# W_in's first half requested earlier, W_spatial later: a newly planned order for a linear-attention and gated-MLP kernel

## The chip, the core and the metric

The kernel runs on one core of a Trainium2 chip. The core has a tensor engine (PE) that does the matmuls, a vector engine (DVE), a scalar engine (ACT), a general engine (POOL) and a sync engine (SP), and it moves data with 16 DMA engines. Each engine works through its own list of instructions in order. The metric is the device time of one launch in microseconds (us). A profile of one execution shows when each instruction ran and what it waited for.

## The reference

`q`, `k`, `v` are (4, 8, 768, 64) in fp32: 4 batches, 8 heads, 768 positions of 64 values. The first part is a linear attention with decay, in blocks of 64 positions; its output is the input of the second part, an MLP whose gate mixes positions.

```python
# attention, per block of 64 positions; state is one 64x64 matrix per head
intra = (qb @ kb.T * Dmask) @ vb                 # Dmask[i, j] = lam**(i-j) for i >= j, else 0
inter = (qb * lam**(pos+1)) @ kv_state
out   = intra + inter
kv_state = lam**64 * kv_state + (kb * lam**(63-pos)).T @ vb
# MLP; x is the attention output as (4, 768, 512)
h = max(x @ w_in, 0)                             # w_in (512, 1024)
u, v = h[..., :512], h[..., 512:]
v_n = (v - mean(v)) / sqrt(var(v) + 1e-6)        # over the 512 features
v_s = w_spatial @ v_n + b_spatial                # w_spatial (768, 768), mixes positions
out = (u * v_s) @ w_out                          # w_out (512, 512)
```

## The kernel before

The work is cut into 12 steps, three per batch; a step is 256 positions of all 8 heads. Every instruction group has a short name, and one list, `ORDER`, written out ahead by a planner, gives the order in which the groups are issued. A token such as `PV.0.1.2.T` is a group (`PV`), its arguments (step 0, part 1, PSUM bank 2) and the engine (T is PE, D is DVE, A is ACT, P is POOL, S is SP). The list is read from left to right and each group goes to the end of its engine's list, so the order on one engine is the order of its tokens. Engines wait for one another only where data or buffers require it. The code of the groups is the same in both kernels; only `ORDER` differs.

The groups that the text speaks of, with the number of the step as n:

- `LQ.n`, `LK.n`, `LV.n` (line 192): SP loads q, k or v of a step, 512 KB each. Each has three buffers (`q_in`, `k_in`, `v_in`, chosen by n modulo 3), so step 3 writes the buffer of step 0.
- `QM.n.x`, `KM.n.x` (289): multiply q or k by powers of lam into bf16 `qc` and `kc`, one half of the heads each, on DVE or POOL. `VC.n` (177, 179 or 181): converts v to bf16. The powers come from `LL` (218, DVE) and `LX` (222 and 223, ACT), and these from `LB` (212, PE) and `LN` (215, ACT).
- `TQ`, `TK` (319): transposes on PE; `EQ`, `EK` copy them out of PSUM. From step 5 on transposing DMAs (`DQ`, `DK`, 306 and 302) do this.
- `SC` (349) scores, `MK` (354) masking on DVE, `KV` (366) state update, `SS` copy of the state, `AV` (387 and 396) attention output in two parts, `FN` a copy of one element that orders the engines, `EX` copies the output, transposed, to `xT`.
- `PV` (421) projects to the second half of W_in's columns, `EV` (426 or 428) applies max, `BN` (436, 437), `RA`, `RD`, `RB` (441, 446, 451) and `VN` (457 or 460) normalise. `PU` (472) and `EU` do the first half of the columns.
- `WT.k.i` (484) transposes W_spatial on PE, where i = 0 reads what `WS.0` loads and i = 1 what `WS.1` loads; `EW` copies it. `GP` puts the bias into PSUM, `PW` (498) mixes positions, `GM` (504) applies the gate, `PO` and `PH` (509 and 518) multiply by W_out, `EO` and `EH` copy to `o_sb`, `ST` and `SH` (532 and 528) store. `BB` and `BE` (258) spread the bias over partitions.
- `WI.j` (243), `WS.j` (248), `WO` (252): POOL requests a half of W_in (j = 0 is the half that `PV` needs), a half of W_spatial, and W_out. These transfers convert fp32 to bf16 as they go; the profile counts the bytes written.
- `GT.x.n` (239): a POOL copy of one element of a load's buffer (x = 0 is k, 1 is q), so that what follows on POOL waits for that load. `HL.1.3` (264): writes one element of the buffer of q of step 3, so that the load `LQ.3` waits for POOL to come there. `GN` (464) does the like with a normalised tile.
- `FL.k.w.b` (272): k matmuls of a tile of ones (`one`, 268, DVE) with w columns, whose result nobody reads.

The two groups with which the list makes POOL and SP wait are one line each:

```python
def after(e, x, n):      # GT
    nc.gpsimd.tensor_copy(out=seen, in_=(k_in, q_in, v_in)[x][n % NIN][0:1, 0, 0, 0:1])
def hold(e, x, n):       # HL
    vec(e).memset((k_in, q_in, v_in)[x][n % NIN][0:1, 0, 0, 0:1], 0.0)
```

In the list before, POOL's tokens up to step 2 are: `msk idn posk QM.0.0 KM.0.0 GT.1.1 WI.0 QM.1.1 VC.0 QM.2.1 WI.1 WS.0 QM.2.0 KM.2.1 KM.2.0 WS.1 HL.1.3 VC.2`. SP's are: `LQ.0 LK.0 LK.1 LQ.1 LV.0 LV.1 LQ.2 LK.2 LV.2 LQ.3 LK.3 LV.3 LQ.4 LK.4`.

Of the kernel before, what the change touches and what calls it, by code (L numbers as in the profile page):

```python
# [31 lines left out]
PU.0.0.5.T EU.0.0.5.A RA.2.A PU.2.0.3.T WT.2.1.1.T EW.2.1.1.D GP.0.0.0.4.A PU.2.1.0.T EU.2.0.3.A WT.1.1.2.T
WT.0.1.6.T RD.2.D VN.2.0.D VN.2.1.D LV.4.S LQ.5.S LK.5.S EU.2.1.0.A GN.2.1.P KM.3.1.P KM.3.0.P PW.0.0.0.4.T
EW.0.1.6.D EW.1.1.2.D GP.0.2.0.5.A GP.0.3.1.3.A TQ.3.2.6.T PW.0.2.0.5.T TK.3.2.1.T GM.0.0.0.4.D EK.3.2.1.D
EQ.3.2.6.A PW.0.3.1.3.T GP.0.1.0.0.A VC.3.P KM.4.0.P GM.0.2.0.5.D SC.3.0.5.6.T SC.3.1.1.2.T GM.0.3.1.3.D
GP.0.3.0.4.A QM.4.0.P QM.4.1.P KV.3.0.T MK.3.0.5.6.D LV.5.S MK.3.1.1.2.D PW.0.3.0.4.T GM.0.3.0.4.D SS.3.0.D
# [535 lines left out]
```

## Time and profile before

| what | value |
|---|---|
| median of 3 runs | 144.38 us (143.93 to 144.56) |
| time of the profiled execution | 143.63 us |
| its span in the profile | 141.9 us |
| PE busy | 132.8 us (94%) |
| DVE, ACT, POOL busy | 110.6, 76.2, 53.5 us |
| read from HBM, written to it | 24.38 MB, 6.29 MB |

The span runs from the first to the last instruction of the profiled execution; the time of that execution holds some 1.7 us more. Busy shares are of the span. A line of the page or of a timeline begins with a start in us, a duration in us, the engine and the line of the code; in square brackets stands the idle time of the engine ahead of it and what ended that. A row of a table of stretches gives the stretch, its length, the busy time of PE, PEld (weight loads of PE), DVE, ACT and POOL with their instruction counts, then the granted PE clock, the mean busy share of the 16 DMA engines and the GB/s that were written. In a list of DMA issues the last number is the median time from the issue to the landing.

### The profile page before, as it was taken

The page shows a single profiled execution, that of the slowest core. Times are in us where ns is not written, and L with a number is a line of the kernel's source. Part 1 is how long each engine was busy: PE and PEld are TensorE (multiplying, and loading weights), DVE is VectorE, ACT ScalarE, POOL GpSimd, SP SyncE. Part 2 cuts the span into 40 slices and gives each one's busy share as a digit, 9 for nine tenths or more (in the row PEclk, how much of TensorE's full clock was granted, in tenths as well). Part 3 has the DMA queues.
Part 4 walks back from the last instruction along what each step waited for, and adds up shares of the span by engine and source line. Part 5 has one row for each costly group of instructions (what it writes and reads, how often), then busy time and mean ns, then how long its engine had stood idle before and what let it go on. Part 6 is the DMA issues. An engine that isn't in the chain of part 4 may idle for free.

```text
span 141.9 us, 4688 instructions
## 1 busy us (share of the span) xinstructions
PE 132.8 (94%) x1980; PEld 86.7 (61%) x1997; DVE 110.6 (78%) x220; ACT 76.2 (54%) x153; POOL 53.5 (38%) x62
## 2 busy tenths in 40 slices
PE   5979979999999999999999999999999999999990
PEld 3855656768577564676566465685665655855550
DVE  3486957998696986697899789977897989984940
ACT  3136748778527666669524647697236642570041
POOL 5567973015997532196715025603700000000000
PEclk9999999999999999999999999999999999999999
DMA  3999999999999999999999899999979242310075
GB/s 84 345 346 345 230 252 210 225 337 257 334 328 239 125 236 343 306 139 347 227 260 158 209 360 241 262 329 165 291 117 259 93 170 98 128 74 0 33 294 191
DMA packets 58232, 31.88 MB, mean 225 GB/s; under 512 B 15843, under 2 KB 55267, under 8 KB 58212
## 3 DMA queue, kind: packets, MB, share of 16 engines
q1 hardware_dynamic: 55824, 28.84, 78.1%
q0 software_dynamic: 2384, 2.75, 11.4%
q8 instruction: 15, 0.25, 0.7%
q14 instruction: 5, 0.04, 0.1%
q10 hardware_dynamic: 4, 0.00, 0.0%
HBM read 24.38 MB, written 6.29 MB: 216 GB/s over the span
## 4 chain that ended last, share of the span: by engine, by line
PE 72%; DMA 14%; DVE 4%; SPq 3%; ACT 2%; issue 1%; POOL 0%; DVEq 0%; ACTq 0%
PE ps L498 21%; PE ps L472 13%; PE ps L509 13%; PE ps L421 13%; DMA win_sb<-in_moe_w_in_dram 7%; DMA q_in<-in_q_dram 4%; DMA v_in<-in_v_dram 3%; PE ps L349 3%; PE ps L396 3%; PE ps L366 3%; DVE a_sb L354 2%; SPq L192 2%; PE ps L319 2%; PE ps L387 1%; SPq L302 1%
## 5 line engine op out<-in xcount | busy, mean ns | idle before, releaser
L498 PE MATMUL ps<-wt_sb,vn 128*128 128x384 bf16 x192 | 34.0, 326 | 0.0
L354 DVE TENSOR_TENSOR a_sb<-ps,m 128x1024 bf16<-128x1024 f32 x24 | 28.6, 1216 | 2.5 <-PE ps L349 1.9
L289 POOL TENSOR_TENSOR kc<-k_in,lv 128x512 bf16<-128x512 f32 x18 | 19.2, 1080 | 22.4 <-DMA k_in<-in_k_dram 6.3
L498 PEld LDWEIGHTS <-vn 128*128 128x128 bf16 x192 | 18.1, 98 | 12.2 <-ACT vn L457 0.4
L289 POOL TENSOR_TENSOR qc<-q_in,lqn 128x512 bf16<-128x512 f32 x19 | 20.0, 1069 | 14.2 <-DMA q_in<-in_q_dram 8.5
L472 PE MATMUL ps<-xT,win_sb 128*128 128x256 bf16 x192 | 23.2, 273 | 0.0
L421 PE MATMUL ps<-win_sb,xT 128*128 128x512 bf16 x89 | 21.8, 379 | 1.2 <-DMA win_sb<-in_moe_w_in_dram 0.6
L509 PE MATMUL ps<-wout_sb,gT 128*128 128x512 bf16 x82 | 21.1, 379 | 1.0 <-issue 0.6
L504 DVE TENSOR_TENSOR gT<-ps,uT 128x384 bf16<-128x384 f32 x32 | 16.8, 551 | 6.0 <-PE ps L498 5.3
L472 PEld LDWEIGHTS <-win_sb 128*128 128x128 bf16 x192 | 18.2, 98 | 3.6
L436 DVE BATCH_NORM_STATS2 st<-vh 128x6 f32<-128x512 bf16 x24 | 16.3, 679 | 0.8 <-ACT vh L426 0.5
L426 ACT ACTIVATE vh<-ps 128x512 bf16<-128x512 f32 x20 | 11.9, 595 | 9.3 <-PE ps L421 9.3
L177 ACT ACTIVATE o_sb<-ps 128x512 f32<-128x512 f32 (+1 forms) x17 | 9.6, 567 | 12.2 <-DVE o_sb L179 8.9
L421 PEld LDWEIGHTS <-xT 128*128 128x128 bf16 x96 | 9.1, 98 | 10.6 <-DVE xT L179 0.7
L509 PEld LDWEIGHTS <-gT 128*128 128x128 bf16 x92 | 8.5, 98 | 9.1 <-DVE gT L504 0.2
L177 ACT ACTIVATE ps<-bsp 128x384 f32<-128x384 f32 x21 | 9.9, 487 | 4.6 <-DVE a_sb L354 3.8
L177 ACT ACTIVATE xT<-ps 128x512 bf16<-128x512 f32 x16 | 9.1, 595 | 4.9 <-PE ps L396 4.9
L181 POOL CAST vb<-v_in 128x1024 bf16<-128x1024 f32 x7 | 7.8, 1118 | 8.1 <-issue 5.3
L396 PE MATMUL ps<-a_sb,vb 64*64 64x128 bf16 x384 | 10.6, 217 | 0.0
L366 PEld LDWEIGHTS <-kc 64*64 64x64 bf16 x320 | 6.8, 109 | 4.9 <-issue 3.8
L426 ACT ACTIVATE uT<-ps 128x512 bf16<-128x512 f32 x16 | 9.2, 586 | 0.4 <-PE ps L472 0.4
L366 PE MATMUL ps<-vb,kc 64*64 64x64 bf16 x320 | 8.6, 194 | 0.4 <-DVE s_sb L179 0.3
...
## 6 DMA issues: line engine op xcount, KB each, us to landing
q_in<-in_q_dram SPq DMA_DIRECT2D x12, 512.0 KB, 6.6
k_in<-in_k_dram SPq DMA_DIRECT2D x12, 512.0 KB, 6.3
v_in<-in_v_dram SPq DMA_DIRECT2D x12, 512.0 KB, 6.2
...
wsp_raw<-in_moe_w_spatial_dram POOLq DMA_DIRECT2D x2, 576.0 KB, 10.2
win_sb<-in_moe_w_in_dram POOLq DMA_DIRECT2D x2, 512.0 KB, 8.9
wout_sb<-in_moe_w_out_dram POOLq DMA_DIRECT2D x1, 512.0 KB, 7.7
...
```

Of the source, the lines that this page charges most:

```text
L177: nc.scalar.activation(out=o, in_=i, func=AF.Copy)
L289: vec(e).tensor_tensor(out=dst[n % NCA][:, u].rearrange("p u m o d -> p o (u m) d"), in0=src[n % NIN].rearrange("p (o u) m d -> p o u m d" ...
L354: nc.vector.tensor_tensor(out=a_sb[n % NA][:, i].rearrange("p o w j x -> p o w (j x)"), in0=ps[:, b0:b1 + 1:b1 - b0].rearrange("p o (w y) ...
L366: nc.tensor.matmul(out=pkv[row(o), u], lhsT=kc[n % NCA][row(c), u, m, o, :], rhs=vb[n % NCA][row(c), 4 * o + u, m, :], start=new and u == ...
L396: nc.tensor.matmul(out=po[c ^ o][row(w), c, i], lhsT=vb[n % NCA][row(c), 4 * o + u, j, :], rhs=a[row(c), i, o, w, j, :], start=(r == 0 and ...
L421: nc.tensor.matmul(out=bank(b), lhsT=x[:, slot(c, g)], rhs=win_sb[:, g, DH:DFF], start=(g == 0), stop=(g == NCH - 1))
L426: nc.scalar.activation(out=o, in_=i, func=AF.Relu)
L436: nc.vector.bn_stats(out=st6[p2][:, t], in_=vh[p2][:, t])
L472: nc.tensor.matmul(out=pu[:, f2].rearrange("p (c x) -> p c x", c=2), lhsT=win_sb[:, g, f * P:(f + 1) * P], rhs=x[:, slot(0, g):slot(1, g) ...
L498: nc.tensor.matmul(out=bank(b)[:, 0:HW], lhsT=vn[bb % 2][:, s, f * P:(f + 1) * P], rhs=wt_sb[:, s, i * HW:(i + 1) * HW], start=False, stop ...
L504: nc.vector.tensor_tensor(out=gT[bb % 2][:, f, cols], in0=bank(b)[:, 0:HW], in1=uT[bb % 2][:, f, cols], op=ALU.mult)
L509: nc.tensor.matmul(out=bank(b), lhsT=gT[bb % 2][:, f, t * P:(t + 1) * P], rhs=wout_sb[:, f, :], start=(f == 0), stop=(f == NCH - 1))
```

## The change

Only `ORDER` changes. The groups are the same but for these: three `FL` groups in place of nine (20 matmuls in place of 47), `GT.0.1` in place of `GT.1.1`, and `RB` for steps 1 and 2 too.

On POOL the tokens up to step 2 are now `msk idn posk HL.1.3 QM.0.1 WI.0 QM.1.0 KM.1.1 QM.1.1 VC.1 WI.1 QM.2.1 GT.0.1 QM.2.0 WS.0 VC.2 WS.1`. `WI.0` no longer follows a read of q of step 1, `HL.1.3` stands ahead of it, behind `QM.0.0` whose buffer it writes, and the two requests for W_spatial stand behind the work on q of step 2, the second behind the conversion of v of step 2. On SP the tokens are now `LK.0 LQ.0 LQ.1 LV.0 LK.1 LV.1 LQ.2 LK.2 LV.2 LK.3 LQ.3 LK.4 LQ.4 LV.3 LV.4`.

On PE the first `PV` now stands ahead of `AV.1`, `KV.1.1` and `TQ.2`. On DVE the memset of the ones (`one`) stands behind `LL`. All later groups are ordered anew on every engine, and some are done by another engine: between DVE and ACT mainly `EO`, `EX`, `EU`, `SS` to ACT.

The beginning of the list before and after:

```diff
--- before.py
+++ after.py
 ORDER = """
-msk.P one.D idn.P FL.6.256.3.1.T LQ.0.S lam.A BR.A tab.0.A row.D LK.0.S FL.2.256.2.1.T LK.1.S LB.6.T LQ.1.S
-FL.16.128.0.1.T LV.0.S LV.1.S FL.6.256.2.0.T posk.P mkc.D LN.6.A LL.D LX.A QM.0.1.D QM.0.0.P KM.0.0.P KM.0.1.D
-TQ.0.0.3.T TQ.0.1.5.T EQ.0.0.3.D TK.0.0.4.T EQ.0.1.5.A EK.0.0.4.A KM.1.0.D TK.0.1.0.T FL.4.256.1.1.T
-FL.5.256.1.0.T KM.1.1.D EK.0.1.0.D GT.1.1.P LQ.2.S WI.0.P QM.1.0.D TK.1.1.1.T SC.0.0.5.6.T TK.1.0.0.T
-SC.0.1.3.4.T LK.2.S EK.1.0.0.A QM.1.1.P MK.0.0.5.6.D FL.6.256.2.0.T TQ.1.0.2.T TQ.1.1.0.T EQ.1.0.2.A EQ.1.1.0.A
-LV.2.S EK.1.1.1.D VC.0.P MK.0.1.3.4.D BB.1.2.T BE.1.2.A FL.1.256.1.0.T SC.1.0.0.1.T SC.1.1.5.6.T KV.0.0.T
-QM.2.1.P MK.1.0.0.1.D MK.1.1.5.6.D WI.1.P AV.0.0.2.3.T FN.0.2.3.A SS.0.0.A VC.1.A BB.0.4.T WS.0.P KV.0.1.T
-AV.0.1.2.3.T BE.0.4.A TQ.2.1.0.T QM.2.0.P SS.0.1.D KM.2.1.P EX.0.1.3.A EX.0.0.2.D KV.1.0.T AV.1.0.1.6.T
-FN.1.1.6.D TQ.2.0.4.T SS.1.0.A AV.1.1.1.6.T KV.1.1.T SS.1.1.D EX.1.0.1.D eps.D EX.1.1.6.A EQ.2.1.0.A EQ.2.0.4.A
-KM.2.0.P PV.0.0.5.T EV.0.0.5.D PV.0.1.2.T EV.0.1.2.A PV.1.0.6.T BN.0.0.D BN.0.1.D TK.2.1.1.T EK.2.1.1.A
-TK.2.0.3.T EK.2.0.3.D EV.1.0.6.A PV.1.1.2.T SC.2.1.0.1.T SC.2.0.4.5.T MK.2.1.0.1.D EV.1.1.2.A tab.1.A
-MK.2.0.4.5.D RA.0.A WS.1.P HL.1.3.P LQ.3.S LK.3.S LV.3.S VC.2.P PU.1.0.3.T PU.1.1.6.T EU.1.0.3.A EU.1.1.6.A
...
+lam.A msk.P LK.0.S tab.0.A LQ.0.S idn.P LQ.1.S mkc.D row.D BR.A posk.P LB.6.T LV.0.S LN.6.A LL.D one.D LX.A
+FL.10.256.6.0.T KM.0.0.D LK.1.S KM.0.1.D QM.0.0.D LV.1.S TK.0.1.4.T HL.1.3.P QM.0.1.P TK.0.0.6.T EK.0.1.4.D
+TQ.0.0.3.T LQ.2.S EK.0.0.6.D WI.0.P TQ.0.1.5.T EQ.0.0.3.A FL.4.256.4.0.T EQ.0.1.5.D QM.1.0.P SC.0.0.3.4.T
+SC.0.1.0.1.T LK.2.S VC.0.A MK.0.0.3.4.D BB.0.6.T KV.0.0.T FL.6.256.2.1.T LV.2.S KM.1.1.P KM.1.0.D SS.0.0.A
+tab.1.A MK.0.1.0.1.D TK.1.0.4.T QM.1.1.P TK.1.1.5.T KV.0.1.T SS.0.1.A VC.1.P TQ.1.1.1.T EK.1.0.4.A LK.3.S
+AV.0.0.0.3.T EQ.1.1.1.D EK.1.1.5.A TQ.1.0.4.T FN.0.0.3.D WI.1.P BE.0.6.A SC.1.1.1.2.T AV.0.1.0.3.T EQ.1.0.4.A
+MK.1.1.1.2.D KV.1.0.T EX.0.0.0.A SC.1.0.4.5.T BB.1.6.T EX.0.1.3.A MK.1.0.4.5.D SS.1.0.A PV.0.1.3.T QM.2.1.P
+PV.0.0.5.T LQ.3.S GT.0.1.P EV.0.1.3.A QM.2.0.P BE.1.6.A BN.0.1.D WS.0.P TQ.2.0.1.T KM.2.1.D AV.1.0.0.4.T
+EQ.2.0.1.A KV.1.1.T KM.2.0.D FN.1.0.4.A AV.1.1.0.4.T LK.4.S TK.2.1.2.T EX.1.0.0.D EX.1.1.4.A TK.2.0.3.T
+TQ.2.1.6.T EV.0.0.5.A EK.2.1.2.D eps.D PV.1.0.1.T EK.2.0.3.D EQ.2.1.6.A BN.0.0.D SC.2.1.3.4.T SC.2.0.5.6.T
+MK.2.1.3.4.D RA.0.A PU.0.1.2.T SS.1.1.A PV.1.1.0.T RD.0.D EU.0.1.2.A MK.2.0.5.6.D VC.2.P PU.0.0.3.T EV.1.1.0.D
+WS.1.P KV.2.0.T AV.2.0.2.4.T BN.1.1.D SS.2.0.A LQ.4.S FN.2.2.4.A EV.1.0.1.A AV.2.1.2.4.T VN.0.0.D BN.1.0.D
+PU.1.0.0.T EX.2.0.2.A EX.2.1.4.A WT.1.0.6.T EU.0.0.3.A PV.2.0.1.T EW.1.0.6.D RA.1.A LV.3.S KM.3.0.P GP.0.2.0.3.D
+WT.0.0.2.T EV.2.0.1.A PV.2.1.6.T KM.3.1.P EU.1.0.0.A BN.2.0.D PU.2.1.4.T EV.2.1.6.A RD.1.D RB.1.D EW.0.0.2.D
+VN.1.0.A TK.3.2.5.T BN.2.1.D WT.2.0.2.T EK.3.2.5.A PU.2.0.1.T EW.2.0.2.D VN.0.1.D RA.2.A PU.1.1.6.T VN.1.1.D
...
 """
```

More of the change, by code (lines that the diff above doesn't have):

```diff
@@ L32 @@
[L32 to L36, printed above, removed]
@@ new lines @@
+PW.2.2.0.3.T GM.2.1.0.4.D GP.2.1.1.2.A VC.10.A PW.2.0.1.6.T GM.2.2.0.3.D GP.2.3.1.5.A KM.10.1.D SC.9.1.3.4.T
+GM.2.0.1.6.D SC.9.0.0.1.T DK.10.S KV.10.0.T MK.9.0.0.1.D PW.2.3.1.5.T GP.2.3.0.6.A SS.10.0.A ST.1.2.S
+PW.2.1.1.2.T MK.9.1.3.4.D ST.1.1.S ST.0.3.S PW.2.3.0.6.T GM.2.1.1.2.D GM.2.3.1.5.D PO.1.3.0.T GM.2.3.0.6.D
+AV.9.0.1.6.T EO.1.3.0.A SC.10.0.2.3.T KV.10.1.T FN.9.1.6.D SC.10.1.4.5.T MK.10.0.2.3.D ST.1.3.S SS.10.1.A
+AV.9.1.1.6.T DK.11.S PO.2.0.0.T VC.11.P EX.9.0.1.D GP.2.2.1.2.A PO.2.2.3.T EO.2.0.0.A EX.9.1.6.D QM.11.0.D
@@ new lines @@
+PV.11.0.1.T RB.9.D EV.11.1.2.D PU.9.1.4.T VN.9.1.A BN.11.1.D EV.11.0.1.A PO.2.5.3.T BN.10.1.D PU.11.0.0.T
+RA.10.A PO.2.3.6.T EO.2.5.3.A RD.10.D BN.11.0.D ST.2.5.S PU.10.1.1.T RB.10.D EO.2.3.6.A VN.10.0.D RA.11.A
+ST.2.3.S PU.11.1.3.T EU.9.1.4.A RD.11.D RB.11.D VN.10.1.D GP.3.1.1.2.A VN.9.0.D PU.9.0.6.T GP.3.1.0.4.A
+VN.11.0.D VN.11.1.D EU.10.1.1.D PW.3.2.0.5.T EU.9.0.6.A GP.3.0.0.1.D EU.11.0.0.A PW.3.1.0.4.T GP.3.3.0.6.A
+GP.3.3.1.0.D GM.3.2.0.5.D PW.3.0.0.1.T GP.3.0.1.5.A EU.11.1.3.A PW.3.3.0.6.T GP.3.2.1.3.A PW.3.3.1.0.T
@@ L84 @@
+GM.3.3.0.6.D GM.3.0.0.1.D PW.3.0.1.5.T GM.3.1.0.4.D PW.3.1.1.2.T GM.3.1.1.2.D GM.3.3.1.0.D PO.3.1.6.T PO.3.2.1.T
+EO.3.2.1.A EO.3.1.6.A ST.3.2.S PW.3.2.1.3.T ST.3.1.S GM.3.0.1.5.D PO.3.0.1.T GM.3.2.1.3.D PO.3.3.0.T EO.3.0.1.A
+ST.3.0.S PO.3.4.6.T EO.3.3.0.D PH.3.5.0.2.T ST.3.3.S EO.3.4.6.A PH.3.5.1.5.T EH.3.5.0.2.D ST.3.4.S EH.3.5.1.5.A
+SH.3.5.0.S SH.3.5.1.S
 """
```

88 lines of the change are left out of this document (38 added, 50 removed).

## The prediction

> **What bounds the kernel now.** I read the page first, then the chain of work that ended last, the stretches microsecond by microsecond, and the timelines of POOL and PE up to 25 us.
>
> ```profile
> PE 132.8 (94%) x1980; PEld 86.7 (61%) x1997; DVE 110.6 (78%) x220; ACT 76.2 (54%) x153; POOL 53.5 (38%) x62
> ```
>
> PE is busy nearly throughout. So the time is the moment at which PE gets its first large product, plus the PE work that is then left, plus stalls, plus the tail. The chain says what sets that moment:
>
> ```profile
> 3.26 6.18 DMA q_in<-in_q_dram
> ...
> 9.49 0.68 POOL seen L239
> 10.17 9.32 DMA win_sb<-in_moe_w_in_dram
> ...
> 19.53 0.38 PE ps L421
> ```
>
> q of step 1 lands at 9.44, GT.1.1 reads it, only then POOL requests W_in's half (WI.0), and 9.32 us later PE starts its first projection (PV, L421). From there PE hardly waits, as the second row below shows (9.95 of 10 us). The other rows show the transfers:
>
> ```profile
> 12.00:13.00 1.00, 0.74 (x5) 0.52 (x6) 1.00 (x1) 0.93 (x2) 1.00 (x2) 1.00 1.14 347
> ...
> 16.00:17.00 1.00, 0.70 (x30) 0.44 (x18) 1.00 (x3) 1.00 (x3) 0.99 (x2) 1.00 1.20 214
> ...
> 20.00:21.00 1.00, 1.00 (x5) 0.45 (x5) 0.51 (x3) 0.32 (x1) 1.00 (x2) 1.00 1.27 207
> ```
>
> ```profile
> 120.00:130.00 10.00, 9.95 (x73) 6.90 (x72) 7.78 (x20) 4.68 (x9) 0.00 (x0) 1.00 0.25 97
> ```
>
> The columns after the clock are the DMA share and the GB/s written. The share is above 1 from 2 to 30 us: the transfers are full, and an earlier one makes another later. Loads alone move 347 GB/s (512 KB in 1.5 us), weights alone 207. POOL's requests:
>
> ```profile
> 10.17 0.94 POOL L243 DMA_DIRECT2D win_sb<-in_moe_w_in_dram  x1
> ...
> 15.18 0.80 POOL L243 DMA_DIRECT2D win_sb<-in_moe_w_in_dram  x1
> 15.97 0.75 POOL L248 DMA_DIRECT2D wsp_raw<-in_moe_w_spatial_dram  x1
> ...
> 20.83 0.80 POOL L248 DMA_DIRECT2D wsp_raw<-in_moe_w_spatial_dram  x1
> ...
> 24.06 1.04 POOL L181 CAST vb<-v_in 128x1024 bf16<-128x1024 f32 x1 [2.34 <-PE ps L349]
> ```
>
> Both halves of W_spatial are requested before v of step 2 is converted (VC.2, 24.06).
>
> **Part 1, WI.0 earlier.** GT.1.1 goes; HL and QM.0.1 now stand in front. In the profile the first load was usable at 4.97 (DVE's first qc) and the second at 6.48 (its first kc). With k first, DVE does KM.0.0 and KM.0.1 from 4.97 to 6.35 (2 x 0.69) and QM.0.0 from 6.48 to 7.17; HL waits for that (0.09), then QM.0.1 on POOL takes 1.05. The request goes out at 8.35 instead of 10.17 (at 8.85 if QM.0.1 takes the 1.54 of POOL's first qc). With the same 9.32 to landing, PV starts at 17.7: -1.8. The ends for that latency are W_out's 7.7 and W_spatial's 10.8. The low end, 16.1, can't be used in full: k of step 1 becomes the fifth load (4.97 + 4 x 1.5 = 11.0), and DVE's KM.1.0 and two masks (0.69 + 2 x 1.22), then AV.0.0, TQ.1.0, SC.1.1, AV.0.1, KV.1.0, SC.1.0 and BB.1 (0.40 + 0.22 + 0.25 + 0.40 + 0.24 + 0.25 + 0.91) bring PE to PV at some 16.5.
>
> **Part 2, work no longer done in the wait.** Before, AV.1 (two parts), KV.1.1 and TQ.2 (two parts) ran ahead of the first PV. Now they stand behind it. By the chain's pieces a part of AV is 0.18 + 0.22, KV 0.24, four transposes 0.22: 0.80 + 0.24 + 0.44 = +1.5. Most of what part 1 wins is work moved, not wait removed.
>
> **Part 3, 27 of 47 fill matmuls gone.** They ran before 14 us in PE's idle time, one behind the last product: 0. What they cover is the PE's pace, a rival below.
>
> **Part 4, step 2 beside the weights.** q, k, v of step 2 were queued mostly ahead of WI.0's bytes; now those come some 2 us earlier, and WI.1 1.0 us earlier (POOL: QM.1.0, KM.1.1 from 11.0, QM.1.1, VC.1, so 14.2). From 14.3 to 19.0 the loads kept (247 GB/s x 4.7 us - 0.52 MB) / 4.7 us = 135 GB/s, 39% of their rate. q, k, v of step 2 and both halves of W_in are 1.57 MB at 347 and 1.05 MB at 207 GB/s, 9.6 us from the moment the sixth load is usable (4.97 + 5 x 1.5 = 12.5): v is usable at 22.1, or at 25.0 if W_spatial's first half (0.59 MB, 2.9 us) gets in between; k near 19 to 20. KM.2.1 and KM.2.0 (0.69 each) now stand on DVE ahead of EX.1.0, which PV.1.0 needs. I take +0.5, between 0 (k early) and 1.2 (both in PE's way, less a transition), because TK.2.1 needs them too. On SP, LK.4 now waits for GT.0.1 (near 17) where LQ.3 waited for HL (21.63); behind it stand LQ.4 and LV.3, and none of these is due before 30: 0. WI.1 itself, needed at 17.7 + 5.0 = 22.7, lands 8.5 after its request, at 22.7.
>
> **Part 5, W_spatial later.** On POOL the order is now QM.2.1, GT.0.1, QM.2.0, WS.0, VC.2, WS.1. So VC.2's wait for v now holds up WS.1, and behind that KM.3, QM.3 and WO. With v at 23.7 (the middle), VC.2 ends at 24.7 and WS.1 is requested then, 3.9 later than before.
>
> ```profile
> wsp_raw<-in_moe_w_spatial_dram POOLq DMA_DIRECT2D x2, 576.0 KB, 10.2
> win_sb<-in_moe_w_in_dram POOLq DMA_DIRECT2D x2, 512.0 KB, 8.9
> wout_sb<-in_moe_w_out_dram POOLq DMA_DIRECT2D x1, 512.0 KB, 7.7
> ```
>
> W_spatial's two took 9.6 and 10.8. I take 9.6: 34.3. Who waits is WT.2.1 and all of PE behind it. From the first PV to KV.2.0 PE has 4 PV and 2 PU (6 x 0.87), AV.1, KV.1.1, TQ.2, TK.2 (1.9) and SC.2 (0.5): 7.6. From KV.2.0 to WT.2.1 it has KV, AV, four PU, two PV, three WT and TK.3: 7.7. WT.2.1 is due at 17.7 + 7.6 + 7.7 + 0.5 = 33.5, a stall of 0.8. With W_out's 7.7 it is 0; with v at 25.0 and 10.8 it is 3.3. The hold that kept step 3's loads behind 21.63 is gone in effect, so loads run beside these bytes; I therefore stay at W_spatial's own rows.
> [...]
>
> **Part 6, the rest newly ordered.** Counted in the order, ACT gains some 7.5 us of copies (EO, EX, EU, SS), DVE loses as much, POOL three passes of about 1.05. None is the bound. From 30 to 130 us PE idles 1.5 us in all, so no more is to be won; a worse order could cost as much. I take 0, bounds -1 to +1.
>
> **Sum.** -1.8 + 1.5 + 0.5 + 0.8 = +1.0. The profiled execution took 143.63 (span 141.9 and 1.7 around it), so 144.6. The median of the runs shown is 0.75 above that: 145.4.
>
> **Rivals.** Half a percent, 0.72 us, is about what a measurement of this kernel tells from no change.
> *Faster:* the weights land sooner after their requests, because fewer bytes are queued ahead of each. It decides at W_in's first half: at 8.1 us or less the first PV is at 16.5, and with WS.1 in time the sum is -3.0 + 1.5 = -1.5, 142.9; at 9.3 it is the next rival. For it: W_in's second half took 8.5 and W_out 7.7. Against: at 8.35 as many loads are queued ahead as at 10.17. 0.28.
> *Nothing:* the first PV at 17.7, but v of step 2 usable at 22.1, so that WS.1 (22.1 + 1.0 + 9.6 = 32.7) lands in time, and k early: -1.8 + 1.5 = -0.3, up to +0.2 with part 4: 144.1 to 144.6. 0.20.
> *The request is not really earlier:* q of step 2 is still requested first (SP did that at 7.93). If HL and QM.0.1 let WI.0 go only at 9.4, part 1 is -0.8: 146.4. 0.06.
> *Cold PE:* the rows below give 236 ns per 256-column fill at first, 128 ns later; the transposes at 6.62 already ran at the later pace. The granted clock reads 1.00 all the while.
>
> ```profile
> 1.53 1.89 PE L272 MATMUL ps<-ones 128*128 128x256 bf16 x8 [1.53 <-DVE ones L268]
> ...
> 6.62 0.62 PE L319 MATMUL ps<-ident,qc 128*128 128x128 bf16 x8
> ...
> 8.59 1.15 PE L272 MATMUL ps<-ones 128*128 128x256 bf16 x9
> ```
>
> So PE ran 5.1 us at half pace. Now the fills wait for "one" behind LL on DVE, to 4.5, and are fewer. If PE is still slow at the first PV, half of 5.1 is lost: 145.4 + 2.5 = 147.9. It decides if the gaps between 7 and 17 us exceed those of before (up to 1.1). Against: from 9 us on the order is dense. 0.08.
> [...]
>
> **How the numbers follow.** My forecast, step 2 and W_spatial late, has 0.38. Slower is 0.38 + 0.06 + 0.08 = 0.52, same 0.20, faster 0.28. The range goes from the fast case with part 6's gain not quite whole, 142.5, to part 5's 3.3 and part 4's 1.2 (144.38 - 0.3 + 4.5 = 148.6). Slower alone would be 145.1 to 148.6.
>
> **What would show it.** WI.0 requested near 8.4, first L421 near 17.7 (wrong: above 18.5). VC.2 near 23.7 and WS.1 behind it, PE waiting at L484 for wsp_raw near 33.5. If L484 waits for nothing and PE's first L498 is before 34.5, parts 4 and 5 are wrong and the kernel is faster.

## The result, and the profile after

| | before | after |
|---|---|---|
| median | 144.16 us (143.37 to 144.56, 4 runs) | 149.01 us (147.82 to 150.02, 4 runs) |
| ratio | | 1.033, 95% interval 1.025 to 1.041 |
| profiled execution, its span | 143.63, 141.9 us | 148.49, 146.8 us |

The kernel is slower, as forecast, but by 4.9 us instead of 1.0, and 0.4 us above the range. Single executions of all kernels scatter by 1 to 2%, now and then more; ratios leave disturbed ones out, and two profiles used below are of their kernel's fastest execution (a_wi_10: 145.82 of up to 149.22 us; b_gt_k: 146.72 of up to 149.85).

PE on the page of the changed kernel: 1.5 us less busy, in a span 4.9 us longer. So all of it is idle time.

```profile
PE 131.3 (89%) x1955; PEld 85.0 (58%) x1970; DVE 110.7 (75%) x211; ACT 83.6 (57%) x167; POOL 48.8 (33%) x59
```

The chain that ended last no longer runs through W_in, but through q of step 2 (`QM.2.1`, `GT.0.1`, `QM.2.0`) and W_spatial's first half:

```profile
17.91 1.03 POOL qc L289
18.94 0.14 POOL seen L239
19.08 0.95 POOL qc L289
20.02 9.83 DMA wsp_raw<-in_moe_w_spatial_dram
...
29.90 0.51 PE ps L484 x6
```

POOL's timeline (start, duration, and in brackets the idle time ahead): W_in's first half is requested 2 us earlier, and everything behind it that needs step 2 stands later.

```profile
8.19 0.93 POOL L243 DMA_DIRECT2D win_sb<-in_moe_w_in_dram  x1
...
14.45 0.80 POOL L243 DMA_DIRECT2D win_sb<-in_moe_w_in_dram  x1
17.91 1.03 POOL L289 TENSOR_TENSOR qc<-q_in,lqn 128x512 bf16<-128x512 f32 x1 [2.65 <-PE ps L421]
...
20.02 0.80 POOL L248 DMA_DIRECT2D wsp_raw<-in_moe_w_spatial_dram  x1
23.83 1.03 POOL L181 CAST vb<-v_in 128x1024 bf16<-128x1024 f32 x1 [3.01 <-DMA v_in<-in_v_dram]
24.82 0.78 POOL L248 DMA_DIRECT2D wsp_raw<-in_moe_w_spatial_dram  x1
```

`QM.2.1` ran at 14.19 before:

```profile
14.19 1.04 POOL L289 TENSOR_TENSOR qc<-q_in,lqn 128x512 bf16<-128x512 f32 x1 [1.04 <-PE ps L349]
```

In both the bracket names PE, but this instruction needs nothing of these products; a run below (a_q2_first) shows that it is the load of q.

PE's timeline: the first PV 2.67 us earlier than before (19.53), then three of the waits that before doesn't have (its only wait for qc is one of 0.3 us). Another, of 0.79 us, is at 37.98 for a normalised tile (L498).

```profile
16.86 1.90 PE L421 MATMUL ps<-win_sb,xT 128*128 128x512 bf16 x7
...
20.13 0.40 PE L319 MATMUL ps<-ident,qc 128*128 128x128 bf16 x4 [1.36 <-POOL qc L289]
...
29.90 0.51 PE L484 MATMUL ps<-ident,wsp_raw 128*128 128x128 bf16 x6 [0.40 <-DMA wsp_raw<-in_moe_w_spatial_dram]
...
92.30 0.44 PE L366 MATMUL ps<-vb,kc 64*64 64x64 bf16 x16 [1.01 <-POOL vb L181]
```

Stretches that answer to those of before (the last three columns are the granted clock, the DMA share and the GB/s written). At 12 us the weights (208) already run where loads alone ran before (347); at 16 us it is the reverse. At the end PE is as busy as before (9.95 of 10 us).

```profile
12.00:13.00 1.00, 0.50 (x12) 0.32 (x12) 0.76 (x1) 0.71 (x1) 1.00 (x2) 1.00 1.22 208
16.00:17.00 1.00, 1.00 (x10) 0.41 (x4) 1.00 (x2) 0.97 (x3) 0.00 (x0) 1.00 1.15 344
20.00:21.00 1.00, 0.87 (x40) 0.77 (x43) 1.00 (x2) 0.39 (x1) 0.82 (x2) 1.00 1.23 208
120.00:130.00 10.00, 9.95 (x91) 6.83 (x91) 8.18 (x26) 6.04 (x14) 0.00 (x0) 1.00 0.42 160
```

The median times from POOL's requests to landing:

```profile
wsp_raw<-in_moe_w_spatial_dram POOLq DMA_DIRECT2D x2, 576.0 KB, 9.3
win_sb<-in_moe_w_in_dram POOLq DMA_DIRECT2D x2, 512.0 KB, 8.8
wout_sb<-in_moe_w_out_dram POOLq DMA_DIRECT2D x1, 512.0 KB, 8.6
```

To see where the time goes I compared the moments at which PE had done equal work: each weight load counted at the steady interval of its matmul, fills at nothing, and the moment at which the sum is reached set against before's. Lag behind before in us (profiled executions):

| before's time | 17.3 | 22.5 | 27.1 | 35.3 | 48.1 | 65.5 | 82.4 | 90.7 | 136 |
|---|---|---|---|---|---|---|---|---|---|
| after | -0.4 | +0.6 | +1.4 | +2.6 | +3.0 | +2.5 | +4.0 | +5.2 | +4.9 |
| a_wi_10 | +0.9 | +0.6 | +1.4 | +1.4 | +1.5 | +1.1 | +2.7 | +2.7 | +2.3 |
| a_wi_11 | +0.7 | +0.4 | +1.2 | +1.2 | +1.4 | +0.9 | +3.0 | +4.2 | +3.8 |
| b_wi_early | +2.7 | +5.1 | +5.1 | +5.3 | +5.3 | +5.1 | +4.9 | +4.9 | +4.9 |
| h_before_after | -0.1 | 0.0 | +1.1 | +1.1 | +2.6 | +2.0 | +1.9 | +2.1 | +2.3 |

The columns at 17.3, 22.5 and 35.3 move by up to 1 us with how the short matmuls are priced, the others by some 0.3. So the loss has two places: 3 us between 17 and 48 us, some 2.5 us between 74 and 91 us (of before's time; 76 to 96 of its own). At 27.1 us the kernels with the new early order lag alike, whether q of step 2 is late (after) or not (a_wi_10, a_wi_11, below); at 48.1 us the two without that delay lag 1.5 us less.

### The profile page after: what moved, and what is told of

Same layout as the page of the kernel before. It is cut to its first block, busy times and chain, and to the rows that moved or that the text cites. A ratio compares the mean times of both kernels' runs of the same rounds, so it can differ in the third digit from the quotient of the medians.

```text
span 146.8 us, 4630 instructions
## 1 busy us (share of the span) xinstructions
PE 131.3 (89%) x1955; PEld 85.0 (58%) x1970; DVE 110.7 (75%) x211; ACT 83.6 (57%) x167; POOL 48.8 (33%) x59
## 4 chain that ended last, share of the span: by engine, by line
PE 51%; DMA 27%; POOL 5%; DVE 5%; SPq 4%; issue 4%; ACT 2%; POOLq 0%
PE ps L498 16%; PE ps L509 9%; PE ps L472 8%; PE ps L421 8%; DMA qT<-qc 7%; DMA wsp_raw<-in_moe_w_spatial_dram 7%; DMA q_in<-in_q_dram 5%; DMA v_in<-in_v_dram 4%; DMA k_in<-in_k_dram 4%; SPq L192 4%; POOL qc L289 3%; PE ps L349 3%; PE ps L366 2%; PE ps L396 2%; DVE vn L460 2%
## 5 line engine op out<-in xcount | busy, mean ns | idle before, releaser
L498 PE MATMUL ps<-wt_sb,vn 128*128 128x384 bf16 x192 | 33.8, 326 | 0.8 <-ACT vn L457 0.8
L289 POOL TENSOR_TENSOR qc<-q_in,lqn 128x512 bf16<-128x512 f32 x18 | 18.6, 1040 | 26.6 <-DMA q_in<-in_q_dram 12.7
L498 PEld LDWEIGHTS <-vn 128*128 128x128 bf16 x192 | 18.2, 98 | 12.6 <-ACT vn L457 1.2
L289 POOL TENSOR_TENSOR kc<-k_in,lv 128x512 bf16<-128x512 f32 x17 | 18.1, 1077 | 18.3 <-PE ps L366 7.8
L421 PE MATMUL ps<-win_sb,xT 128*128 128x512 bf16 x89 | 22.2, 379 | 0.6 <-DVE xT L179 0.3
L177 ACT ACTIVATE o_sb<-ps 128x512 f32<-128x512 f32 (+1 forms) x21 | 12.2, 586 | 15.5 <-PE ps L509 15.1
L177 ACT ACTIVATE xT<-ps 128x512 bf16<-128x512 f32 x20 | 11.0, 595 | 7.3 <-PE ps L396 7.0
L177 ACT ACTIVATE ps<-bsp 128x384 f32<-128x384 f32 x23 | 11.0, 494 | 6.8 <-DVE a_sb L354 4.3
L421 PEld LDWEIGHTS <-xT 128*128 128x128 bf16 x96 | 9.0, 98 | 10.0 <-ACT xT L177 1.1
L426 ACT ACTIVATE vh<-ps 128x512 bf16<-128x512 f32 x18 | 10.6, 594 | 6.4 <-PE ps L421 6.2
L426 ACT ACTIVATE uT<-ps 128x512 bf16<-128x512 f32 x19 | 10.8, 592 | 2.6 <-PE ps L472 2.3
L177 ACT ACTIVATE s_sb<-ps 128x256 bf16<-128x256 f32 x18 | 6.8, 381 | 6.6 <-PE ps L366 6.5
L181 POOL CAST vb<-v_in 128x1024 bf16<-128x1024 f32 x6 | 6.2, 1042 | 13.0 <-issue 6.7
L396 PE MATMUL ps<-a_sb,vb 64*64 64x128 bf16 x384 | 10.2, 217 | 0.3 <-DVE a_sb L354 0.3
L349 PE MATMUL ps<-qT,kT 64*64 64x128 bf16 x384 | 9.0, 219 | 0.8 <-DMA qT<-qc 0.7
```

Of the source, the lines that this page charges most:

```text
L177: nc.scalar.activation(out=o, in_=i, func=AF.Copy)
L289: vec(e).tensor_tensor(out=dst[n % NCA][:, u].rearrange("p u m o d -> p o (u m) d"), in0=src[n % NIN].rearrange("p (o u) m d -> p o u m d" ...
L349: nc.tensor.matmul(out=pa[o][row(c), w, j], lhsT=kT[n % NTR][row(o), u, j, c * Q64:(c + 1) * Q64], rhs=qv(n, o, u, c), start=(w == 0 and j ...
L396: nc.tensor.matmul(out=po[c ^ o][row(w), c, i], lhsT=vb[n % NCA][row(c), 4 * o + u, j, :], rhs=a[row(c), i, o, w, j, :], start=(r == 0 and ...
L421: nc.tensor.matmul(out=bank(b), lhsT=x[:, slot(c, g)], rhs=win_sb[:, g, DH:DFF], start=(g == 0), stop=(g == NCH - 1))
L426: nc.scalar.activation(out=o, in_=i, func=AF.Relu)
```

## The experiments

Kernels named a_ are the changed kernel with one edit, b_ the kernel before with one edit, h_ are put together from both orders. The diffs show one engine's tokens. The ratios are to the kernel before on the same chip.

### W_spatial's request or W_in's

**a_ws_ahead.** W_spatial's requests forward.

```diff
 POOL
-VC.1 WI.1 QM.2.1 GT.0.1 QM.2.0 WS.0 VC.2 WS.1
+VC.1 WI.1 WS.0 QM.2.1 GT.0.1 QM.2.0 WS.1 VC.2
```

> The changed kernel with both requests for W_spatial moved forward on POOL: WS.0 directly behind WI.1 (near 15.3 us instead of 20.0), WS.1 in front of VC.2 (near 20.5 instead of 24.8). Theory S, the late W_spatial costs the time up to 40 us: WT.1.0 no longer waits and PE reaches its first L498 about 1 us earlier; 147.5 to 148.5 us. Theory B, the DMA engines are full and what is late is q, k and v of step 2: W_spatial's bytes now go ahead of v, VC.2 runs at 25 to 26.5 instead of 23.8; 149.0 to 151 us.

Measured: 149.84 us, ratio 1.036 (1.027 to 1.045). The requests went out at 15.05 and 19.80, and v of step 2 came 1.9 us later than in the changed kernel:

```profile
25.68 1.03 POOL L181 CAST vb<-v_in 128x1024 bf16<-128x1024 f32 x1 [5.07 <-DMA v_in<-in_v_dram]
```

W_spatial's late request is not what costs: made 5 us earlier (20.02 and 24.82 in the changed kernel), it went with a later v and no shorter time.

**a_wi_10.** W_in's first half one POOL pass later.

```diff
 POOL
-QM.0.1 WI.0 QM.1.0 KM.1.1
+QM.0.1 QM.1.0 WI.0 KM.1.1
```

> The changed kernel with WI.0 one place later on POOL, behind QM.1.0, so that it is requested near 10.2 us as before the change. Theory B: q of step 2 lands some 2 us earlier (QM.2.1 near 16 instead of 17.9), TQ.2.0 no longer waits 1.4 us, the first L421 starts near 19 instead of 16.9; what the early request won is what q of step 2 lost, so 148.5 to 149.5 us. Theory E, the early request is good and the rest of the new order is bad: 150.5 to 151 us.

Measured: 147.98 us, ratio 1.014 (1.002 to 1.026). The request 0.9 us later, q of step 2 2.7 us earlier, and no wait at L319 for q of step 2:

```profile
9.09 0.93 POOL L243 DMA_DIRECT2D win_sb<-in_moe_w_in_dram  x1
...
15.21 1.05 POOL L289 TENSOR_TENSOR qc<-q_in,lqn 128x512 bf16<-128x512 f32 x1
```

**b_wi_early.** The early request alone, in the kernel before.

```diff
 POOL
-KM.0.0 GT.1.1 WI.0 QM.1.1
+KM.0.0 WI.0 QM.1.1
```

> The kernel before with one part of the change alone: GT.1.1 left out and WI.0 directly behind KM.0.0 on POOL (near 8.1 us instead of 10.2). Everything else keeps its old order. Theory E: the first L421 starts near 17.5 and nothing is moved behind it, 142.7 to 143.3 us. Theory B: q, k and v of step 2 come 1 to 3 us later, and TQ.2, which stands ahead of the first PV in this order, holds PE; first L421 not before 19.5, 144 to 145.5 us.

Measured: 149.49 us, ratio 1.037 (1.027 to 1.046). Leaving out one token gives a loss as large as the changed kernel's, all of it by 28 us, though not by the same steps: part of it is the clock, as the next run shows. q of step 2 comes 3.7 us later than in before:

```profile
17.85 1.04 POOL L289 TENSOR_TENSOR qc<-q_in,lqn 128x512 bf16<-128x512 f32 x1 [5.89 <-DMA q_in<-in_q_dram]
```

and PE, which waits 2.42 us for it at L319, also works at a granted clock of 0.50 (third column from the right) from 15.8 to 26.1 us:

```profile
16.00:18.00 2.00, 0.54 (x19) 0.29 (x8) 1.43 (x3) 1.08 (x3) 0.15 (x1) 0.50 1.15 345
...
22.00:24.00 2.00, 1.87 (x43) 1.43 (x43) 0.56 (x2) 1.06 (x3) 2.00 (x3) 0.50 1.23 206
```

**b_wi_early_fl.** The same, with fills where PE is idle.

```diff
 PE
-AV.0.1 TQ.2.1
+AV.0.1 FL.22.256 TQ.2.1
```

> The kernel before with WI.0 early as in the run on that part alone, and 22 fill matmuls of 256 columns (2.4 us at full pace) put on PE behind AV.0.1, where it waited 2.4 us for q of step 2 and the granted clock then fell to 0.5 until 26 us. Theory C, most of that run's 5 us is the clock: it stays at 1.00, the first L421 is near 22.5 and PE is 2.5 to 3 us ahead of that run by its first L498; 146.3 to 147.2 us. Theory N, the time is q's lateness alone and PE's pace doesn't matter there: 149 to 150 us.

Measured: 148.21 us, ratio 1.027 (1.023 to 1.031). The granted clock is back at 1.00 from 20 us on (from 26.1 in b_wi_early), and the lag at 25 us is 3.0 instead of 5.1: some 2.1 us were the clock, 3.0 are q. Less of it lasts to the end than I expected: the medians differ by 1.3 us.

**a_tq_later.** Work put where PE waits for q.

```diff
 PE
-PV.0.0 TQ.2.0 AV.1.0 KV.1.1 AV.1.1
+PV.0.0 AV.1.0 KV.1.1 AV.1.1 TQ.2.0
 ACT
-EQ.2.0 FN.1.0
+FN.1.0 EQ.2.0
```

> The changed kernel with TQ.2.0 (the first product that needs q of step 2) two places later on PE, behind AV.1, and its copy EQ.2.0 behind it. Theory Q, PE's wait of 1.4 us for q of step 2 is itself on the path: the AV.1 parts fill it, the wait at L319 near 19 falls to 0.4 us or less, 0.8 to 1.2 us less than the changed kernel, 147.8 to 148.3 us. Theory D, with full DMA engines the next late arrival (k, v of step 2, W_in's second half) takes its place: less than 0.4 us changes, 148.6 to 149.4 us.

Measured: 148.23 us median (145.98 to 149.97), too scattered for a ratio. The lag at 27 us is 1.1 instead of 1.4, at the end 4.7: little is won.

**a_q2_first.** The loads of v of step 1 and q of step 2 exchanged on SP.

```diff
 SP
-LK.1 LV.1 LQ.2 LK.2
+LK.1 LQ.2 LV.1 LK.2
```

> The changed kernel with q of step 2 and v of step 1 exchanged in SP's order, so that W_in's bytes begin while v of step 1 is on its way. Theory V, the load in whose bytes W_in's request begins is the one that is held up: QM.2.1 runs near 15 instead of 17.9, and VC.1 near 16 to 18 instead of 13.5, so that KV.1.0 and with it the first PV wait, first L421 at 18 to 19.5; 149 to 151 us. Theory W, q of step 2 is late for the sum of the bytes whatever the order: QM.2.1 still near 17 or later, VC.1 near 13 to 14, time within 0.7 us of the changed kernel.

Measured: 153.17 us, ratio 1.060 (1.056 to 1.065). q of step 2 makes nobody wait now; v of step 1, which took its place in SP's queue, is 4 us later:

```profile
17.46 1.04 POOL L181 CAST vb<-v_in 128x1024 bf16<-128x1024 f32 x1 [3.99 <-DMA v_in<-in_v_dram]
```

So the victim is whichever load stands in that place (q in the changed kernel, converted at 17.91, v at 17.46 here), and the wait for `QM.2.1` was its load. (The 1.060 is not this delay alone: PE waits 3.05 us for v at `KV.1.0`, and the granted clock reads 0.50 from 18.2 to 25.0.)

### The moment of the request

SP's timeline of the changed kernel; the second column is the time SP needs to issue the load:

```profile
7.92 1.45 SPq L192 DMA_DIRECT2D q_in<-in_q_dram  x1
9.41 1.45 SPq L192 DMA_DIRECT2D k_in<-in_k_dram  x1
```

These places (7.8 to 9.3 for q of step 2, 9.3 to 10.9 for k) are the same within 0.2 us in all these kernels. Three runs move the request in the kernel before, by what stands ahead of `WI.0` on POOL.

```diff
 POOL
-KM.0.0 GT.1.1 WI.0 QM.1.1
+KM.0.0 GT.0.1 WI.0 QM.1.1    b_gt_k
+KM.0.0 KM.1.0 WI.0 QM.1.1    b_km_pool (KM.1.0 was on DVE)
+KM.0.0 QM.1.1 WI.0           b_gt_drop
```

> The kernel before, GT reading k of step 1 (the third load) instead of q of step 1 (the fourth): W_in's first half is requested near 8.8 instead of 10.2, nothing else changed. At 7.9 the same kernel took 148.6, with q of step 2 converted at 17.9. Theory V (the load that is in flight when the request begins is held up): q of step 2 converted at 17 or later if its bytes still run at 8.8 (then 146 to 148), near 15 if most are through (then PE's wait of 0.6 for W_in goes and the time is 143.0 to 143.6). The changed kernel with the request at 9.1 had it at 15.2, so I expect the second, 143.6 or less, with 0.6; with the first, PE waits over 1 us at L319 for qc.

> The kernel before without GT.1.1; in its place on POOL stands KM.1.0 (it stood on DVE), which waits for k of step 1 and takes 1.05 to 1.5 us, so that W_in's first half is requested near 9.4 (10.17 before), behind the 7.85 to 9.3 in which SP's queue issues the load of q of step 2. Theory V2 (only the loads not yet issued at the request are held up): q of step 2 converted near 14.2 as before, first PV near 18.8 instead of 19.5, the wait of 0.6 for W_in gone: 143.0 to 143.4 in the profiled run, ratio 0.995 to 1.0. Theory W (every earlier request is paid for, by k and v of step 2 if not by q): PE waits for kc of step 2 or loses it elsewhere, 143.9 or more, ratio 1.003 to 1.02 (a request at 8.6 gave 1.033, one at 9.1 in the changed kernel 1.014).

> The kernel before without GT.1.1, W_in's first half behind the conversion of q of step 1 on POOL (QM.1.1): requested near 10.5 instead of 10.2, while POOL's qc and vb of step 1 come 0.6 us earlier. Earlier requests cost 5.1 us at 7.9 and 3 us at 8.6. Theory V (a request costs what it holds up of step 2's loads): q of step 2 is converted no later than before (14.2) and W_in's half lands 0.3 later, 143.6 to 144.1 or a little under (k of step 2 not held up): no change. Theory P (W_in's half itself sets the time): +0.3 to +0.4, 144.0. Either way no more than 0.5% from before; what tells them apart is the wait at L421 for win_sb (0.6 in before) and the moments of qc and kc of step 2.

| kernel | request | q of step 2 converted | first PV | ratio (95%) |
|---|---|---|---|---|
| b_wi_early | 7.92 | 17.85 | 23.26 | 1.037 (1.027 to 1.046) |
| b_gt_k | 8.56 | 16.35 | 21.76 | 1.033 (1.028 to 1.038) |
| b_km_pool | 9.34 | 13.99 | 19.65 | 0.995 (0.992 to 0.999) |
| before | 10.17 | 14.19 | 19.53 | 1 |
| b_gt_drop | 10.90 | 14.06 | 20.27 | 1.004 (1.001 to 1.008) |

```profile
8.56 0.94 POOL L243 DMA_DIRECT2D win_sb<-in_moe_w_in_dram  x1
...
16.35 1.04 POOL L289 TENSOR_TENSOR qc<-q_in,lqn 128x512 bf16<-128x512 f32 x1 [4.36 <-PE ps L396]
```

A request early or midway in SP's issue of q of step 2 (7.92, 8.19, 8.56) delays q by 2 to 3.7 us; one sent right behind it (9.34) leaves q alone. The place on SP is only a pointer, though: a_wi_10 asks at 9.09, 0.2 us before that issue is over, and q is not late there. The DMA packets in the traces show what decided here. The first packets of W_in's half run 3.4 to 4.2 us after the request: at 11.6 to 11.7 us in b_wi_early and the changed kernel, 12.7 in b_gt_k, 13.0 in b_km_pool and a_wi_10, 14.3 in before. q of step 2, the seventh load, has its last packets at 13.2 to 13.4 in before, b_gt_drop, b_km_pool and a_wi_10, at 14.8 in b_gt_k, and at 16.2 in b_wi_early and the changed kernel. Here is the changed kernel from 12 to 13 and from 13 to 14 us: packets, MB written, share of the 16 DMA engines. q0 is the queue of POOL's requests and q1 that of SP's loads; a packet of W_in writes 1 KB, one of a load 512 bytes.

```profile
q0 software_dynamic: 188, 0.19, 114.9%
q1 hardware_dynamic: 31, 0.02, 7.2%
...
q0 software_dynamic: 140, 0.14, 84.0%
q1 hardware_dynamic: 142, 0.07, 35.5%
```

So q's load nearly stands still for 1 us and then moves at a fifth of its rate (0.07 MB in 1 us, where loads alone move 0.35).

b_km_pool is the only kernel here that beats before (144.08 us against 144.64). Part of the price in b_wi_early and b_gt_k is the clock: b_gt_k's profiled execution has 3.4 us at half clock and took 146.72 us, the others have mean clocks of 0.965 to 0.977 and took 148.21 to 149.85. b_gt_k missed my expectation: q was not "mostly through". In b_gt_drop the request is later than planned (`QM.1.1` took 1.60) and PE waits 1.45 us for W_in, 0.74 us of lag; but k of step 2, whose place was over at 10.73, is now converted with no wait ahead, 1.8 us earlier than in b_km_pool (19.38):

```profile
17.61 2.05 POOL L289 TENSOR_TENSOR kc<-k_in,lv 128x512 bf16<-128x512 f32 x2
```

b_km_pool's profiled execution shows where its gain is lost in part: PE waits for nothing in the 4 us before its first PV, but works at half clock (granted 0.50) from 15.8 to 19.2.

```profile
9.34 0.94 POOL L243 DMA_DIRECT2D win_sb<-in_moe_w_in_dram  x1
...
13.99 1.04 POOL L289 TENSOR_TENSOR qc<-q_in,lqn 128x512 bf16<-128x512 f32 x1 [1.67 <-DMA q_in<-in_q_dram]
```

```profile
16.00:17.00 1.00, 1.00 (x22) 0.63 (x14) 1.00 (x3) 1.00 (x3) 0.99 (x2) 0.50 1.14 270
```

### Hold and W_spatial by themselves

**b_nohold** drops `HL.1.3` from the kernel before; **b_ws_late** moves its W_spatial requests.

```diff
 POOL, b_ws_late
-WI.1 WS.0 QM.2.0 KM.2.1 KM.2.0 WS.1 HL.1.3 VC.2
+WI.1 QM.2.0 WS.0 KM.2.1 KM.2.0 HL.1.3 VC.2 WS.1
```

> The kernel before with the hold of step 3's loads (HL.1.3) dropped and nothing else: q of step 3 no longer waits for a write at 21.6, only for its buffer (q of step 0, converted by 7.2), and k and v of step 3 follow it. Theory N (what the prediction took: no cost): within 0.5% of before. Theory D (the transfers are full, so step 3's loads take bandwidth from W_in's second half and W_spatial, and q, k, v of step 2 are already through): W_in's second half or W_spatial land 1 to 3 us later, PE waits at L421 or L484, 144.8 to 146.5.

> The kernel before with W_spatial's first half requested behind both QM.2 (near 17.7 instead of 16.0) and its second half behind the conversion of v of step 2 (near 25.1 instead of 20.8): part 5 of the change alone. By the prediction's part 5: 25.1 + 9.6 = 34.7 against a first use that the trace of before has at about 33: PE waits 0.8 to 1.7 at L484 for wsp_raw, 144.4 to 145.3 in the profiled run. Theory R (W_spatial's lateness costs nothing, its bytes only stand in the way of others): the time stays or falls (143.0 to 143.8), because q, k, v of step 2 come sooner, and the bytes behind 25 us find less in front of them.

Measured: b_nohold 144.77 us, ratio 1.001 (0.998 to 1.005); b_ws_late 145.27 us, ratio 1.002 (0.998 to 1.006). In the profiled executions both show the wait that was to come, b_nohold 1.0 us at PU (for W_in's second half) and b_ws_late 1.36 us at `WT.2.1`:

```profile
PE ps L472 <- DMA win_sb<-in_moe_w_in_dram: 1.0, 1, 1.0
```

```profile
34.78 0.51 PE L484 MATMUL ps<-ident,wsp_raw 128*128 128x128 bf16 x6 [1.36 <-DMA wsp_raw<-in_moe_w_spatial_dram]
```

Over twelve runs they cost at most 0.7 and 0.8 us (the intervals' upper ends). Neither is the loss.

### The second place, 74 to 91 us

**a_late** moves a little of the order of steps 7 to 9, **a_sp_late** gives SP the order that before has there.

```diff
 POOL
-QM.6.1 KM.7.1 KM.7.0 QM.8.0 QM.7.0
+QM.6.1 KM.7.1 KM.7.0 QM.7.0 QM.8.0    a_late
+QM.6.1 QM.7.0 KM.7.1 KM.7.0 QM.8.0    a_sp_late
 SP
-DQ.6 LV.8 LK.9 DK.7 DQ.7 LQ.9 LK.10 DK.8 ST.0.5 DQ.8 LQ.10 LV.9
+DQ.6 LV.8 LK.9 DK.7 DQ.7 LQ.9 LK.10 LV.9 DK.8 ST.0.5 DQ.8 LQ.10    a_late
+DQ.6 DQ.7 LK.9 DK.7 LV.8 LV.9 LQ.9 DK.8 DQ.8 LK.10 LQ.10 ST.0.5    a_sp_late
```

> The changed kernel with two tokens of the later steps moved: QM.7.0 in front of QM.8.0 on POOL, and LV.9 in front of DK.8 on SP. Theory L, the 2 us lost between 78 and 93 us come from the new order of these queues (the transpose of q of step 7 issued behind a product for step 8 that waits for a buffer; v of step 9 issued behind the transposes of step 8): waits at L349 near 78 and 86 and at L366 near 92 go, 147.0 to 147.6 us. Theory K, they are a consequence of the lateness up to 40 us: less than 0.5 us changes, 148.5 to 149.5 us.

> The changed kernel with SP's order for steps 7 to 9 much as before the change (both transposes of step 7 directly behind that of q of step 6, v of step 9 ahead of the transposes of step 8) and QM.7.0 early enough on POOL for it. Theory L2, the 2 us lost between 78 and 93 us come from SP's order: no wait at L349 near 78 and none at L366 near 92, 1.5 to 2.2 us less than the changed kernel, 146.8 to 147.5 us. Theory K, that stage is late because the transfers are full and the start was late: another wait takes their place, less than 0.5 us changes.

Measured: a_late 148.68 us, ratio 1.028 (1.020 to 1.037); a_sp_late 149.78 us, ratio 1.041 (1.034 to 1.048). In both the wait for v of step 9 goes, and others of 1 to 2 us come in its place (L349 for qT 2.0 and L498 for vn 1.0; L396 for a_sb 1.5 and L498 for vn 1.0).

**h_before_after** and **h_after_before**: one kernel's order up to `GM.0.2.1` (47 to 50 us), the other's from there.

> The order of the kernel before up to the last product of the first half with W_spatial (GM.0.2.1, near 47 us), from there the order of the changed kernel; the same work in both parts, no bank changed. The changed kernel fell 2.4 us behind by 50 us and another 2.6 us between 76 and 95 us. Theory O (the later order is slow in itself): the second loss comes without the first, 143.6 + 2.6 = 146.2 in the profiled run, with waits at L349, L396 or L366 between 75 and 95 us. Theory C (the second loss is a consequence of the first part's lateness): within 0.5 us of before, 143.1 to 144.2.

> The reverse: the order of the changed kernel up to GM.0.2.1 (near 50 us), from there the order of the kernel before. Theory O: only the first part's 2.4 us remain, 143.6 + 2.4 = 146.0. Theory C: the loss of 2.6 us after 75 us stays, 148.5. If the later order of before even absorbs the lag (its loads come sooner in relation to PE), under 146.

Measured: h_before_after 144.49 us, ratio 0.999 (0.996 to 1.003); h_after_before 152.57 us, ratio 1.056 (1.051 to 1.062). The later order of the changed kernel costs nothing behind the early order of before, even in a profiled execution (145.79) that is itself 2 us late by 65 us. Its rows for 84 to 96 us (PE's busy time is the first number behind the length):

```profile
84.00:90.00 6.00, 5.95 (x142) 3.59 (x133) 5.00 (x10) 4.57 (x11) 2.92 (x3) 1.00 1.19 269
90.00:96.00 6.00, 6.00 (x82) 4.47 (x81) 4.32 (x12) 5.01 (x12) 3.21 (x4) 1.00 1.20 257
```

The same stretches of the changed kernel:

```profile
84.00:90.00 6.00, 5.31 (x112) 2.94 (x112) 5.29 (x9) 3.03 (x6) 1.04 (x1) 1.00 1.05 291
90.00:96.00 6.00, 4.93 (x103) 3.50 (x103) 4.08 (x10) 4.17 (x9) 3.59 (x4) 1.00 1.16 273
```

So neither the later order alone nor a lag of 2 us makes the second loss; it comes with what the early order leaves behind. The reverse hybrid, with the order of before from 50 us, is worse still: one wait of 3.67 us for the state copy (line numbers are 2 lower in the hybrids).

```profile
58.87 0.63 PE L364 MATMUL ps<-vb,kc 64*64 64x64 bf16 x16 [3.67 <-ACT s_sb L175]
```

### Parts 1 and 2 undone in the changed kernel

**a_wi_10_av** and **a_wi_11_av** put the work of part 2 back ahead of the first PV; **a_wi_11** and a_wi_11_av wait for v of step 0 ahead of the request.

```diff
 POOL
-QM.0.1 WI.0 QM.1.0 KM.1.1
+QM.0.1 QM.1.0 WI.0 KM.1.1           a_wi_10_av
+QM.0.1 QM.1.0 GT.2.0 WI.0 KM.1.1    a_wi_11, a_wi_11_av
 PE, a_wi_10_av and a_wi_11_av
-PV.0.1 PV.0.0 TQ.2.0 AV.1.0 KV.1.1 AV.1.1
+AV.1.0 KV.1.1 AV.1.1 PV.0.1 PV.0.0 TQ.2.0
 ACT, the same two
-EV.0.1 BE.1 EQ.2.0 FN.1.0
+FN.1.0 EV.0.1 BE.1 EQ.2.0
```

> The changed kernel with W_in's first half requested behind QM.1.0 (9.1 instead of 8.2) and with AV.1.0, FN.1.0, KV.1.1 and AV.1.1 put back ahead of the first PV. With the request alone at 9.1 the first PV waited 0.98 us for W_in at 18.2 and the profiled run took 145.8. Theory M (part 2 of the prediction: work moved out of the wait costs its full time): the 1.04 us fit into that wait, PV still near 18.2, profiled run 144.8, within 0.5 us of before by 30 us. Theory F (the wait was filled in other ways, or the order behind it takes the gain back): 145.5 to 146.5.

> The changed kernel with W_in's first half requested behind QM.1.0 and a wait for v of step 0 (GT.2.0), near 10.2 as in the kernel before: part 1 of the change undone. Theory V2: q of step 2 no later than 15.2 (its value with the request at 9.1), PE waits some 2 us for W_in, first PV near 19.4, and the 1.04 us of AV.1 and KV.1.1 that stand behind it come on top: some 1.5 us behind before at 30 us, 145.1, ratio 1.01. If the loss after 75 us (2.6 in the changed kernel, 1.4 with the request at 9.1) is a consequence of lateness, it is 1 to 1.5 again: 146.5, ratio 1.02.

> The same with AV.1.0, FN.1.0, KV.1.1 and AV.1.1 put back ahead of the first PV: parts 1 and 2 undone, all else as in the changed kernel (hold dropped, W_spatial later, the new order). Theory V2: the early stage is that of before, within 0.5 us at 30 us, first PV near 19.4, and the whole is 143.6 to 144.6, ratio 0.998 to 1.007. If the other parts together do cost (hold, W_spatial and the order were free only one by one), 145 to 147, ratio 1.01 to 1.02. The PE's granted clock may fall in the gap ahead of the first PV (it did with the request at 9.1): then up to 2 us more.

Measured: 150.07 us, ratio 1.035 (1.028 to 1.042); 148.95 us, ratio 1.024 (1.018 to 1.030); 149.69 us, ratio 1.033 (1.028 to 1.038). v of step 0 had landed sooner than I thought, so the request went out at 9.57, not 10.2; q was converted at 15.27, as in a_wi_10, and the second loss is in the lag table above. With the work put back, the granted clock fell to 0.50 in the profiled executions (17.7 to 21.1 in a_wi_10_av) and PE then waited for kc of step 2 (1.1 us there). So theory M fell, and none of the kernels with the new early order reached before's time. By the ratios a later request gives back 1.3 (a_wi_11) to 2.8 us (a_wi_10) of the 4.7, but their intervals overlap the changed kernel's (1.025 to 1.041). a_wi_11_av missed its expectation widely. With the request at 9.48 and `QM.2.1` at 15.20 its early stage was to be that of before within 0.5 us at 30 us; by the count of equal work it is some 3 us late at 27 us. Its 3.4 us at half clock (19.3 to 22.7) explain at most 1.7 of these, as PE does half the work at a granted 0.50 (5 products of L421 from 24 to 26 us in b_wi_early, 10 from 20 to 22 in before at 1.00), and its one execution at full clock took 149.96 us all the same. So the new early order costs PE something besides q's delay, 1.2 to 1.5 us by 27 us in these kernels, and no run here isolates what.

## Why the prediction was right and wrong

- **Part 1** held: the request at 8.19 (8.35 forecast; its terms add up to 8.31), the first PV at 16.86, at its lower end, not at 17.7. That end was given as 16.5, but its terms (11.0, 3.13 on DVE, 2.67 on PE) add up to 16.8, just what was measured. W_in came 8.67 us after its request or sooner. Where PE did wait for it, it took 8.4 to 9.5 (a_wi_11, a_wi_10, before, b_gt_drop, b_ws_late).
- **Part 2** held in direction: the first PV is 2.67 us earlier, the equal work at most 0.4 us. Putting the work back did not bring that back, so its +1.5 is not shown by itself.
- **Part 3** held in the changed kernel: the granted clock stays at 1.00. *Cold PE* fell there; but a granted 0.50 came in b_wi_early (15.8 to 26.1 us), where PE also stood idle for q, at 2.1 us (2.5 in the rival).
- **Part 4** is the step that failed. It gave k and v of step 2 a moment each and q none; a rival even has q ahead of W_in, because SP requests it first. The request went out in the middle of q's place on SP; q came 3.7 us later (17.91), PE waited 1.36 us for it at `TQ.2.0`, and WS.0, which stands behind `QM.2.0` on POOL, went out at 20.02. The term was +0.5. By b_wi_early_fl the delay of q is worth 3.0 in the kernel before. In the changed kernel, 3.0 late at 48 us, it costs 1.5 more than the earlier first PV wins: a_wi_10 and a_wi_11, which have the new order without the delay and a first PV 1.1 to 1.3 us later, are 1.5 and 1.4 late there. What makes these 1.5 stays open. k and v themselves came as worked out: k landed at 19.23 (19 to 20), VC.2 ran at 23.83 (23.7).
- **Part 5** named a wait that is real but not due here. WS.1 went out at 24.82 (24.7). Alone, in b_ws_late, `WT.2.1` waits 1.36 us at 34.78, inside the 0.8 to 1.7 expected of it. In the changed kernel PE comes to `WT.2.1` at 35.71, 2.2 us later than forecast, and waits for nothing there; +0.8 was counted beside a delay that covers it.
- **Part 6** (0, -1 to +1) was the other term that failed: between 65.5 and 90.7 us of the lag table it is 2.7 in the changed kernel, 1.6 in a_wi_10 and 3.3 in a_wi_11. ACT gained 7.4 us of work as counted, but DVE lost none (110.7 against 110.6). The later order is worth 0 behind before's early order, so no work was left out of it. It failed in holding the late stage independent of the early one. What hands the loss on stays open: the changed kernel has one load fewer issued when the later order begins (v of step 5), and SP's queue then runs 2.9 us behind that of h_before_after at 60 us and 4.1 at 82; but no run isolates this.
- The rival *Faster* had its condition nearly met (PV at 16.86) and still did not come: it, too, left q out. With the measured values for parts 1 and 5 (-2.7 and 0) the forecast's own sum would be -0.7, faster. So that it was right in sign is in part luck: the reason, step 2 late, it had only in part.
